# Attention and a gated feed-forward block on one core: adding two of the three terms of an approximated exponential on VectorE, with a new order plan

## The chip, the core and the metric

One core of a Trainium2 chip runs the kernel. The metric is the device time of one execution in microseconds. The kernel before has a median of 750.6 us over three runs (750.47 to 752.39).

The core has five engines, and the program gives each a queue of its own, in a fixed order: PE (TensorE, matrix multiplications from SBUF into PSUM), ACT (ScalarE, activation functions such as exp and tanh), DVE (VectorE, elementwise arithmetic), POOL (GpSimd) and SP (SyncE, which here only starts DMAs). The kernel uses PSUM as eight banks of 128 x 512 fp32 values (the tile PS).

## The reference

```python
# A_x: 1 x 2048 x 512, 32 heads of width 16; F = 1792
qkv = layernorm(A_x) @ A_wqkv
p = softmax(q @ k.T * 16 ** -0.5)          # per head, 2048 x 2048
h = A_x + (p @ v) @ A_wo
n = layernorm(h)
h2 = h + (sigmoid(n @ B_w_gate) * (n @ B_w_up)) @ B_w_down
```

The matrices of scores of the 32 heads have 2048 x 2048 x 32 elements, and each of them needs an exponential. That is most of what ACT does. The product with the values and the scores themselves are most of what PE does.

## The kernel before

**The unit of work.** A unit is a stretch of scores of 128 x 512 elements of one head: 128 keys on the partitions and 512 queries, or two blocks of 128 keys (SPAN is 2) and 256 queries. There are 2048 units. PE computes the scores of two or three units of one tile at once into neighbouring PSUM banks (`scores`, matmul at L1087): a head is only 16 wide, so the matmuls of different heads lie side by side in the array. There are 695 tiles. PE writes the scores of tile n+1 while tile n is turned into exponentials; the bank numbers alternate by the table PLACES (L1019), so scores of tile n+1 wait for those that read tile n-1.

**Two ways to an exponential.** Of each tile, ACT takes all units or all but one, in one activation of 512, 1024 or 1536 columns (L1415), and writes fp16 values into a place of the tile pt (or into other buffers that are free just then: xnT, QTb, xb, pe). The last unit of the tile can go to DVE (`dexp_first`, L1252): one tensor_scalar (L1258) writes a 16-bit integer whose bits, read as fp16, are a first approximation of the exponential. Two units share one buffer J (GQ is 2; six such buffers, QB). When both are there, `dexp_rest` (L1270) makes two further values of each from the first by adding an integer constant to the bits (the two "chords", CHORDS): POOL does this for both units at once as an int64_add over packed words (`chord64`, L1278), before POOL is free for it DVE does it (`chord`). The exponential is the sum of the three fp16 values, the last weighted by 1.5625 (through Vaug2, values that are weighted beforehand).

**The product with the values.** A unit of ACT is one row of value matmuls; a unit of DVE is three rows, since each of the three fp16 values is multiplied with the values (Vaug or Vaug2) and summed in PSUM (`av`, L1213, matmul at L1235). With SPAN 2 a row is two matmuls of 256 columns. The 17 columns of Vaug (16 values and a half for the row sum) are narrow, so the rows of four heads lie side by side, and four rows take the time of one. `avq` is the list of rows that wait, `todo` the number of rows still due for each head of a group; when it reaches zero, `finish_group` (L1113) transposes, divides by the row sum and transposes back on DVE.

**The rest of PE's work.** The projections of q, k and v, the product with A_wo and the feed-forward block (L826 gate and up, L844 down) are cut in pieces of two or four matmuls and put between the attention tiles (`try_bg`, L961), as fast as tokens come in. Where PE would be idle for too long, `stir` (L651) adds a matmul whose result nobody reads.

**What sets the order.** The kernel's Python code writes every queue out in one order while the program is built. It keeps a clock for each engine (T["P"], T["A"], T["D"], T["G"]) and books a cost for every instruction: 216 ns for a pass of PE, 112 for a change between kinds of matmul, for ACT 51 and 426.5 for each unit. Work for DVE, ACT and POOL waits as a `Job` (L523) until what it depends on is booked as done; `run_dve` (L599) picks the next job of DVE, `run_pool` (L552) that of POOL. In the main loop (L1377) each tile has an activation, perhaps a DVE unit, and then steps in which PE gets value rows or a dense piece. The dictionary PLAN (L23, 92 entries) overrides single choices: key 16 * tile + step forces what PE does in a step (1 to 3: so many rows of values, 4: a dense piece, 5: leave 100 ns, 9: end the tile), key + 15 forces (2) or forbids (1) a DVE unit, key + 14 chooses which head it takes.

**The tail** (L1487 on). After the last tile the remaining value rows, a first part of the last product with A_wo (identity part L1506, L1509), the last values, the last layernorm and the last feed-forward chunk follow: 14 steps of gate and up (L826), tanh (L856) and product (L839), then the down matmuls (L1584) and the output. At the very end three DVE instructions (L1593 to L1598) check all row sums for being in range, a matmul and a copy make one flag of it (L1601, L1603), and each engine reads the flag and branches: a general kernel follows if it is set, which it is not here.

Of the kernel before, what the change touches and what calls it, by code (L numbers as in the profile page):

```python
# [8 lines left out]
FP32 = mybir.dt.float32  # L9
# [13 lines left out]
PLAN = {414: 2, 528: 5, 656: 5, 672: 2, 736: 4, 737: 3, 750: 2, 769: 9, 801: 2, 815: 1, 817: 2, 1198: 3, 1200: 3, 1201: 3, 1376: 1, 1409: 3, 1423: 1, 1472: 9, 1473: 5, 1474: 4, 1601: 9, 1634: 3, 1682: 4, 1696: 9, 1713: 4, 1840: 9, 1857: 5, 1872: 4, 1873: 1, 1890: 9, 1938: 1, 2033: 1, 2047: 1, 2144: 5, 2145: 2, 2161: 2, 2384: 2, 2417: 4, 3728: 3, 3730: 4, 4240: 1, 4255: 1, 4321: 3, 4353: 4, 4367: 2, 4752: 2, 4753: 5, 4767: 2, 6112: 5, 6129: 3, 7040: 3, 7041: 3, 7696: 4, 7711: 1, 7713: 4, 7742: 2, 7761: 9, 7904: 2, 8512: 4, 8513: 3, 8913: 1, 8926: 3, 8928: 2, 8930: 1, 8943: 2, 8944: 4, 8960: 3, 8975: 1, 9200: 3, 9393: 4, 9410: 4, 9889: 4, 9890: 3, 9952: 2, 9984: 3, 10000: 2, 10178: 3, 10302: 2, 10528: 3, 10543: 2, 10640: 1, 10687: 2, 10703: 2, 10848: 4, 10894: 2, 10945: 1, 10959: 2, 11023: 1, 11089: 4, 11102: 1, 11103: 1, 11106: 1}  # L23
# [121 lines left out]
def kernel(  # L145
# [376 lines left out]
    T = {e: max(0.0, free[e] - tasks["go"].end) for e in free if e != "N"}  # L522
    class Job:  # L523
        def __init__(self, ns, fn, deps):
            self.ns, self.fn, self.deps, self.end = ns, fn, [d for d in deps if d is not None], None
# [5 lines left out]
        def place(self, eng):  # L531
            T[eng] = max(T[eng], self.ready()) + self.ns
            self.end = T[eng] + TAIL[eng]
            self.fn()
            if eng != "G":
                run_pool()
# [715 lines left out]
    def dexp_first(src, u, n):  # L1252
        if not half:
            half.append(dvx.tile([P, 3, GQ, QC], I16, name="J", bufs=QB))
            quads.append([])
        J = half[0]
        k = len(half) - 1
        nc.vector.tensor_scalar(out=J[:, 0, k, :], in0=src, scalar1=ZOFF, scalar2=float(-min(CHORDS)),  # L1258
                                op0=ALU.add, op1=ALU.max)
        T["D"] = max(T["D"], sc_end[n] + LAT) + 601  # L1260
        todo[u[0], u[1], u[3]] += 2
        uns = [Unit(u, J[:, s, k, :].bitcast(FP16), n, None if s else T["D"] + TAIL["D"],
                    v=Vaug2 if s == 2 else Vaug) for s in range(3)]
        avq.extend(uns)
        half.append(uns)
        quads[-1].extend(uns)
        if k == GQ - 1:
            dexp_rest()

    def dexp_rest():  # L1270
# [7 lines left out]
        def chord64(s):  # L1278
            nc.gpsimd.int64_add(words(s), words(0), CHORDS[s - 1] * (1 + 2 ** 16 + 2 ** 32 + 2 ** 48))  # L1279
            for i in range(k):  # L1280
                quad[i][s].end = T["G"] + TAIL["G"]
# [10 lines left out]
        for s in (1, 2):  # L1292
            if on_pool:
                pool(150 + 192 * k, lambda s=s: chord64(s), Mark(T["D"] + TAIL["D"]))
# [206 lines left out]
    while any(un.n < N - 1 and un.slot is not None for un in avq):  # L1501
        flush()
        av(8, 1e12)
    nc.scalar.activation(out=small.tile([P, 1], FP32, name="warm")[:], in_=eps_t[:], func=ACT.Sqrt)
    for i in range(n):
        nc.tensor.matmul(hps[i], lhsT=ident2[:], rhs=xl[:, i, :], start=True, stop=False)  # L1506
    for p in range(NP - 1):
        for i in range(n):
            nc.tensor.matmul(hps[i], lhsT=OT[qc, p][:, i * P:(i + 1) * P], rhs=wo_sb[:, p, :],  # L1509
                             start=False, stop=False)  # L1510
    T["P"] += MM * n * NP
# [12 lines left out]

    while avq:
        flush()
        av(8, 1e12)
    flush()
    mv = small.tile([P, n, nc.vector.BN_AGGR_DIM], FP32, name="mvl")
# [46 lines left out]
    hT = fpool.tile([P, FC, PW], BF16, name="hT")  # L1576
    for f in range(FC):
# [3 lines left out]
        glu_out(hT, f, tanh_out(g_ps[:, 0:CW[qc]]), u_ps[:, 0:CW[qc]])  # L1581
    for i in range(n):
        for f in range(FC):
# [6 lines left out]
    bad = small.tile([P, 1], FP32, name="bad")  # L1590
    okay = work.tile([P, S // 32 * NG], FP32, name="xs")
    rs = rsum[:]
    nc.vector.tensor_scalar(out=okay[:], in0=rs, scalar1=2 / SUM_HIGH, scalar2=None, op0=ALU.is_ge)  # L1593
    nc.vector.scalar_tensor_tensor(out=okay[:], in0=rs, scalar=2 / SUM_LOW, in1=okay[:],
                                   op0=ALU.is_le, op1=ALU.mult)
    nc.vector.tensor_reduce(out=bad[:], in_=okay[:], axis=AX.X, op=ALU.min)
    badb = small.tile([P, 1], BF16, name="badb")
    nc.vector.tensor_scalar(out=badb[:], in0=bad[:], scalar1=-1.0, scalar2=1.0, op0=ALU.mult, op1=ALU.add)  # L1598
    ones1 = small.tile([P, 1], BF16, name="ones1")
    nc.vector.memset(ones1[:], 1.0)  # L1600
    nc.tensor.matmul(acc[0:1, 0:1], lhsT=ones1[:], rhs=badb[:], start=True, stop=True)  # L1601
    flag = const.tile([1, 1], I32, name="flag")
    nc.vector.tensor_copy(out=flag[:], in_=acc[0:1, 0:1])  # L1603
# [34 lines left out]
```

## Time and profile before

| | |
|---|---|
| median of three runs | 750.6 us |
| the profiled execution | 750.78 us |
| span from its first to its last instruction | 749.0 us |
| PE busy, matmuls | 714.2 us, 11497 instructions |
| ACT busy | 710.6 us, 788 |
| DVE busy | 617.5 us, 1223 |
| POOL busy | 392.4 us, 715 |
| int64_add on POOL (L1279) | 646, mean 592 ns |
| first step of a DVE unit (L1258) | 611, mean 681 ns |
| activation of 128 x 1024 into pt (L1415) | 466, mean 1085 ns |
| granted TensorE clock | 0.998 |

Busy times add up the durations of single instructions. Instructions of one engine overlap in part: the next one starts before the profile calls the one before it ended, and up to four matmuls of narrow tiles run side by side. So a share of 95% doesn't say that the engine could do no more; the distance from start to start of two instructions that follow each other without a wait says what one of them costs. The first exponential starts at 13.06 us, the last ends at 714.68 us; what follows is the tail.

### The profile page before, as it was taken

The page shows a single profiled execution, that of the slowest core. Times are in us where ns is not written, and L with a number is a line of the kernel's source. Part 1 is how long each engine was busy: PE and PEld are TensorE (multiplying, and loading weights), DVE is VectorE, ACT ScalarE, POOL GpSimd, SP SyncE. Part 2 cuts the span into 40 slices and gives each one's busy share as a digit, 9 for nine tenths or more (in the row PEclk, how much of TensorE's full clock was granted, in tenths as well). Part 3 has the DMA queues.
Part 4 walks back from the last instruction along what each step waited for, and adds up shares of the span by engine and source line. Part 5 has one row for each costly group of instructions (what it writes and reads, how often), then busy time and mean ns, then how long its engine had stood idle before and what let it go on. Part 6 is the DMA issues. An engine that isn't in the chain of part 4 may idle for free.

```text
span 749.0 us, 27149 instructions
## 1 busy us (share of the span) xinstructions
PE 714.2 (95%) x11497; PEld 346.0 (46%) x11571; DVE 617.5 (82%) x1223; ACT 710.6 (95%) x788; POOL 392.4 (52%) x715
## 2 busy tenths in 40 slices
PE   8999998888999999999999999999999999999986
PEld 3322223444454445544555455535544455455554
DVE  7987898788988888898999678977889778898843
ACT  8988999999999999999999999999999999999952
POOL 2733556666565545664555545555564555566500
PEclk9999999999999999999999999999999999999999
DMA  7000005000132003311122123201321133003350
GB/s 239 1 1 1 1 2 170 2 3 3 31 101 76 20 10 101 87 31 30 45 63 68 37 65 99 61 9 39 101 58 37 31 93 115 10 10 87 97 173 18
DMA packets 68927, 41.65 MB, mean 56 GB/s; under 512 B 3520, under 2 KB 68800, under 8 KB 68800
## 3 DMA queue, kind: packets, MB, share of 16 engines
q1 hardware_dynamic: 68512, 39.59, 18.0%
q8 instruction: 92, 1.51, 0.9%
q14 instruction: 35, 0.29, 0.1%
q10 hardware_dynamic: 288, 0.26, 0.1%
HBM read 37.75 MB, written 2.10 MB: 53 GB/s over the span
## 4 chain that ended last, share of the span: by engine, by line
PE 71%; ACT 18%; DVE 6%; issue 4%; DMA 0%; POOL 0%; DVEq 0%; ACTq 0%; POOLq 0%
PE PS L1087 24%; PE PS L1235 22%; PE PS L826 13%; ACT pt L1415 12%; PE PS L844 5%; DVE J L1258 3%; PE PS L318 2%; ACT xnT L1415 2%; PE PS L765 2%; PE PS L313 2%; ACT pe L1415 1%; DVE xs L1153 1%; PE PS L1584 1%; ACT xb L1415 1%; ACT th L856 1%
## 5 line engine op out<-in xcount | busy, mean ns | idle before, releaser
L1279 POOL INT64_ADD J<-J x646 | 374.1, 592 | 303.4 <-DVE J L1258 253.0
L1415 ACT ACTIVATE pt<-PS 128x1024 f16<-128x1024 f32 (+1 forms) x516 | 520.8, 1119 | 9.2 <-PE PS L1235 4.8
L1258 DVE TENSOR_SCALAR J<-PS 128x512 int16<-128x512 f32 x611 | 408.4, 681 | 76.6 <-PE PS L1087 43.4
L1087 PE MATMUL PS<-QT,KT 32*128 32x256 bf16 (+1 forms) x3712 | 263.7, 276 | 13.6 <-ACT pt L1415 8.0
L1235 PE MATMUL PS<-J,Vaug 128*17 128x256 f16 (+1 forms) x3486 | 238.2, 279 | 2.0 <-DVE xs L1153 1.1
L1235 PE MATMUL PS<-pt,Vaug 128*17 128x256 f16 (+1 forms) x2049 | 195.6, 279 | 1.3 <-DVE xs L1153 1.0
L1087 PEld LDWEIGHTS <-KT 32*128 32x128 bf16 x3840 | 88.6, 92 | 197.7 <-issue 193.8
L1235 PEld LDWEIGHTS <-Vaug 128*17 128x17 bf16 x6164 | 138.4, 90 | 88.2 <-issue 82.5
L826 PE MATMUL PS<-xnT,wgu 128*128 128x256 bf16 x784 | 113.0, 275 | 0.2 <-DVE ob L850 0.2
L1415 ACT ACTIVATE xnT<-PS 128x1024 f16<-128x1024 f32 (+1 forms) x89 | 97.8, 1128 | 0.2
L826 PEld LDWEIGHTS <-wgu 128*128 128x128 bf16 x784 | 63.8, 98 | 38.9 <-issue 33.6
L1235 PE MATMUL PS<-xnT,Vaug 128*17 128x256 f16 x368 | 54.4, 273 | 0.0
L844 PE MATMUL PS<-wd,hT 128*128 128x512 bf16 x171 | 51.7, 383 | 2.3 <-issue 2.2
L1415 ACT ACTIVATE QTb<-PS 128x1024 f16<-128x1024 f32 x42 | 45.8, 1090 | 0.6 <-PE PS L1087 0.6
L856 ACT ACTIVATE th<-PS 128x512 f32<-128x512 f32 (+1 forms) x63 | 38.5, 612 | 7.9 <-DVE hT L839 6.1
L898 DVE SCALAR_TENSOR_TENSOR hT<-th,PS 128x512 bf16<-128x512 f32 x49 | 33.3, 680 | 6.2 <-PE PS L826 6.1
L1153 DVE STREAM_TRANSPOSE xs<-PS 128x256 f32<-128x256 f32 (+1 forms) x60 | 27.7, 461 | 10.8 <-PE PS L1235 10.3
L1235 PE MATMUL PS<-QTb,Vaug 128*17 128x256 f16 (+1 forms) x166 | 27.5, 275 | 0.4 <-DVE xs L1153 0.4
L1415 ACT ACTIVATE xb<-PS 128x1024 f16<-128x1024 f32 (+2 forms) x26 | 26.1, 1034 | 1.9 <-PE PS L1087 1.3
L1124 DVE TENSOR_TENSOR o<-xs,rsum 128x128 bf16<-128x128 f32 (+1 forms) x60 | 24.5, 408 | 2.1
L1415 ACT ACTIVATE pe<-PS 128x1024 f16<-128x1024 f32 (+2 forms) x22 | 21.9, 1068 | 1.5 <-PE PS L1235 0.9
L844 PEld LDWEIGHTS <-hT 128*128 128x128 bf16 x196 | 12.3, 97 | 20.8 <-issue 17.5
(128 smaller groups left out, 394.7 us busy)
## 6 DMA issues: line engine op xcount, KB each, us to landing
wgu<-in_B_w_gate_dram SPq DMA_DIRECT2D x49, 256.0 KB, 3.0
wgu<-in_B_w_up_dram SPq DMA_DIRECT2D x49, 256.0 KB, 3.4
out_dram<-ob SPq DMA_DIRECT2D x16, 128.0 KB, 1.7
wd<-in_B_w_down_dram SPq DMA_DIRECT2D x1, 1792.0 KB, 7.6
xr<-in_A_x_dram SPq DMA_DIRECT2D x14, 128.0 KB, 3.7
xb<-in_A_x_dram SPq DMA_DIRECT2D x6, 256.0 KB, 6.5
J<-in_B_w_gate_dram SPq DMA_DIRECT2D x4, 384.0 KB, 6.0
J<-in_B_w_up_dram SPq DMA_DIRECT2D x4, 384.0 KB, 6.8
```

Source lines behind the costliest of these rows:

```text
L313: nc.tensor.matmul(ps, lhsT=w_sb[:, d, p * P:(p + 1) * P], rhs=xnT[c][:, d, :], start=(d == 0), stop=(d == DC - 1))
L826: nc.tensor.matmul(ps[:, 0:PARTS[r][2]], lhsT=w[:, d, :], rhs=hn_of(r)[:, d, :], start=(d == 0), stop=(d == DC - 1))
L844: nc.tensor.matmul(ps, lhsT=hT[:, f, i * P:(i + 1) * P], rhs=wd[:, f, :], start=(f == 0), stop=(f == FC - 1))
L856: nc.scalar.activation(out=th[:, 0:ps.shape[-1]], in_=ps, func=ACT.Tanh, scale=0.5)
L898: nc.vector.scalar_tensor_tensor(out=hT[:, f:f + k, 0:w], in0=th[f][:].rearrange("p (k n) -> p k n", k=k), scalar=1.0, in1=ps2.rearrange(" ...
L1087: nc.tensor.matmul(pss[:, ui, i * CW[qc]:(i + 1) * CW[qc]], lhsT=KT[g // 2][32 * j:32 * j + 32, k * P:(k + 1) * P], rhs=q[32 * j:32 * j + ...
L1124: nc.vector.tensor_tensor(out=o2[:, 0:w // 32, DH * a:DH * a + DH], in0=xs[:, 0:w // 32, 0:DH], in1=rec.to_broadcast([P, w // 32, DH]), op ...
L1153: j = dve(650 - ns[0], lambda: nc.vector.transpose(out=xs[:, 0:w // 32, :].rearrange("p b r -> p (b r)"), in_=src), Mark(T["P"] + DRAIN), ...
L1235: nc.tensor.matmul(dst[32 * j:32 * j + VW, 0:w], lhsT=un.v[:, kt * SPAN[qc] + i, h, :], rhs=un.ap[:, i * w:(i + 1) * w], start=clears and ...
L1258: nc.vector.tensor_scalar(out=J[:, 0, k, :], in0=src, scalar1=ZOFF, scalar2=float(-min(CHORDS)), op0=ALU.add, op1=ALU.max)
L1279: nc.gpsimd.int64_add(words(s), words(0), CHORDS[s - 1] * (1 + 2 ** 16 + 2 ** 32 + 2 ** 48))
L1415: ex = nc.scalar.activation(out=pt, in_=pss[:, 0:wa, :], func=ACT.Exp, scale=AS)
```

## The change

Where a pair of DVE units goes to POOL, and DVE's list of ready jobs is empty at that moment (or PLAN says so: key + 12, 1 for yes and 2 for no), the pair's first value is added to the second on DVE, as an fp16 tensor_tensor over 1024 columns (512 for a single unit). The row of the first value is taken out of `avq` and of `todo`, so such a unit has two rows of value matmuls. POOL makes the second chord before the first for such a pair, and the add waits for the first. The value of the add is booked as ready when it is done; the first value of a pair without an add is now booked as ready when the pair is complete, not when it is written.

The bookkeeping learns that an add of DVE and an int64_add of POOL exclude each other (`lock`, `spans`, `holds`): each is booked behind the other if they would overlap. PLAN is new and has 354 entries over the whole run.

In the tail, the eight dense matmuls (identity and A_wo, now a list `fill`) no longer come ahead of the last value rows: rows that are ready go first, and the list fills the waits. The three checks of the row sums go between the steps of the last feed-forward chunk (after steps 2, 4, 6 and 8), the flag's matmul and copy after step 10.

```diff
         def place(self, eng):
-            T[eng] = max(T[eng], self.ready()) + self.ns
+            at = max(T[eng], self.ready())
+            if eng == "G":
+                for a, b in holds:
+                    if a <= at < b:
+                        at = b
+                spans.append((at, at + self.ns))
+            elif self.lock:
+                for a, b in spans:
+                    if a <= at + 40 and at < b - 150:
+                        at = b - 150
+                holds.append((at, at + self.ns))
+            T[eng] = at + self.ns
...
-        uns = [Unit(u, J[:, s, k, :].bitcast(FP16), n, None if s else T["D"] + TAIL["D"],
+        uns = [Unit(u, J[:, s, k, :].bitcast(FP16), n, None,
...
+        busy = sum(j.ns for j in dq if j.ready() is not None) + sum(c[0] for c in chain)
+        both = on_pool and (PLAN.get(16 * st["n"] + 12, 0) == 1 or PLAN.get(16 * st["n"] + 12, 0) == 0 and (busy == 0))
+        if both:
+            for uns in quad:
+                u = uns[0].u
+                avq.remove(uns[0])
+                todo[u[0], u[1], u[3]] -= 1
+
+            def add():
+                f1 = J[:, 1, 0:k, :].bitcast(FP16)
+                nc.vector.tensor_tensor(out=f1, in0=f1, in1=J[:, 0, 0:k, :].bitcast(FP16), op=ALU.add)
+                for uns in quad:
+                    uns[1].end = T["D"] + TAIL["D"]
+        else:
+            for uns in quad:
+                uns[0].end = T["D"] + TAIL["D"]
-        for s in (1, 2):
+        for s in (2, 1) if both else (1, 2):
             if on_pool:
-                pool(150 + 192 * k, lambda s=s: chord64(s), Mark(T["D"] + TAIL["D"]))
+                j = pool(150 + 192 * k, lambda s=s: chord64(s), Mark(T["D"] + TAIL["D"]))
+                if both and s == 1:
+                    dve(70 + 264 * k, add, j, pr=2).lock = True
...
-    while any(un.n < N - 1 and un.slot is not None for un in avq):
-        flush()
-        av(8, 1e12)
...
+    flush()
     while avq:
-        flush()
-        av(8, 1e12)
+        if av(8, 120.0):
+            flush()
+        elif fill:
+            fill.popleft()()
+            pe_time("dense", MM)
+        else:
+            flush()
+            av(8, 1e12)
...
+        if f in checks:
+            checks[f]()
+        if f == 10:
+            nc.tensor.matmul(acc[0:1, 0:1], lhsT=ones1[:], rhs=badb[:], start=True, stop=True)
+            nc.vector.tensor_copy(out=flag[:], in_=acc[0:1, 0:1])
```

## The prediction

> **What bounds the kernel now.** First the head of the page and its chain:
>
> ```profile
> PE 714.2 (95%) x11497; PEld 346.0 (46%) x11571; DVE 617.5 (82%) x1223; ACT 710.6 (95%) x788; POOL 392.4 (52%) x715
> ...
> PE 71%; ACT 18%; DVE 6%; issue 4%; DMA 0%; POOL 0%; DVEq 0%; ACTq 0%; POOLq 0%
> ```
>
> Two engines claim 95%, and the chain names mostly PE. A busy share can't settle it, so I read a stretch of the timeline, by start times:
>
> ```profile
> 300.12 0.62 PE L1235 MATMUL PS<-J,Vaug 128*17 128x256 f16 x16
> 300.68 0.40 PE L1087 MATMUL PS<-QT,KT 32*128 32x256 bf16 x6
> ...
> 301.57 0.40 PE L1087 MATMUL PS<-QT,KT 32*128 32x256 bf16 x6
> 301.90 0.61 PE L826 MATMUL PS<-xnT,wgu 128*128 128x256 bf16 x4
> 302.44 0.40 PE L1087 MATMUL PS<-QT,KT 32*128 32x256 bf16 x6
> ```
>
> and the same stretch on ACT:
>
> ```profile
> 301.15 1.94 ACT L1415 ACTIVATE pt<-PS 128x1024 f16<-128x1024 f32 x2
> 302.96 1.04 ACT L1415 ACTIVATE xnT<-PS 128x1024 f16<-128x1024 f32 x1
> 303.86 0.63 ACT L856 ACTIVATE th<-PS 128x512 f32<-128x512 f32 x1
> 304.34 4.74 ACT L1415 ACTIVATE pt<-PS 128x1024 f16<-128x1024 f32 x5
> ```
>
> ACT: from 301.15 to 302.96 it does two exponentials over 1024 columns, 0.905 us each; the tanh at 303.86 takes 0.48. Over the whole trace the commonest distances are 903, 1330 and 476 ns for 1024, 1536 and 512 columns, and these are also the smallest: ACT back to back. PE: scores take 0.33 us (one pass of 512 columns, 213 ns, and 112 for the switch of shape), four gate matmuls 0.54 (two passes and a switch), 16 value matmuls 0.56 (four run side by side, so two passes and 132 ns). A tile with two passes beside its scores thus takes 0.87 to 0.89 us of PE, and its exponential 0.90 of ACT. Both engines are nearly full.
>
> I priced every tile by these numbers, in the instruction order of both programs (us, tiles by number; the last tile of PE with its scores alone, what follows is the tail):
>
> | tiles | PE before | ACT before | PE after | ACT after |
> |---|---|---|---|---|
> | 0-74 | 72.3 | 67.3 | 71.1 | 68.2 |
> | 75-199 | 103.5 | 115.2 | 100.5 | 116.1 |
> | 200-449 | 248.2 | 246.3 | 242.7 | 245.4 |
> | 450-694 | 241.2 | 242.5 | 235.6 | 240.4 |
> | sum | 665.2 | 671.3 | 650.0 | 670.0 |
>
> The exponentials run from 13.06 to 714.68 us, 701.6. ACT needs 671.3 of it: 30.3 us are stalls, 13.7 before 200 us and 16.6 after. One kind is visible:
>
> ```profile
> 272.26 1.45 ACT L1415 ACTIVATE pt<-PS 128x1536 f16<-128x1536 f32 x1 [1.79 <-PE PS L1235]
> ```
>
> The exponential had no free place for its result, because PE was behind with the value matmuls that empty the places (L1344). PE's backlog becomes ACT's stall.
>
> **What the Trainium skill says.** "Perfetto Trace Analysis", in its opening note on judging how close a kernel is to roofline, calls matmul busy time a bad metric since matmuls are pipelined. The trace agrees: a gate matmul shows 275 ns, yet four of them and their switch pass in 540. "VectorE: DVE Perf Modes", The perf-mode tier table, gives a 16-bit tensor_tensor in SBUF at most two elements a cycle, 1224 ns for 2048; its side-by-side section splits that into some 158 cycles fixed and half a cycle per element. My estimate from that page for 1024: 670 cycles at 0.96 GHz, 0.70 us shown. No such row stands in this trace. "SBUF — State Buffer", Who interferes with whom: a VectorE instruction with two SBUF inputs and a GpSimd instruction that reads SBUF exclude each other, and the later one waits for all of the earlier. The trace has the sister case (a copy-like instruction, one input):
>
> ```profile
> L326 DVE TENSOR_SCALAR QT<-qd,mask x28: 328/344/747, 73.8 to 575.3; 128x512 bf16<-128x512 bf16 x28
> ```
>
> Alone it takes 344 ns; those that meet a running int64_add take up to 747, so a collision costs up to 0.4 us.
>
> **The change part by part.** ACT gets no new kind of work. The plan of the order grows from 92 to 354 entries, so every tile's place can shift; the table has that in it.
>
> *Value rows.* The new order holds 102 adds (92 over two units, 10 over one), so 194 of 614 VectorE units lose a row. Value matmuls fall from 6164 to 5810; in passes of 512 columns, four abreast, 812.25 to 762.5. 49.75 x 213 ns = 10.6 us of PE saved. Two warming matmuls less: 0.4. The new plan also groups PE's work in longer runs: 35 fewer groups (668 runs of scores instead of 674, 696 others instead of 725) at 112 to 132 ns, 4 us. Together 15, as the table's sums say.
>
> *Units.* VectorE takes 614 instead of 611, ACT 1434 instead of 1437: 1.3 us of ACT (the table).
>
> *Conversion.* ACT's 670 stays below everything, so PE's 15 us count only where PE is late. Scores run one tile ahead, thus PE and ACT can lag each other by some tiles. If I cut the order in groups of consecutive tiles and take the larger engine of each group, three tiles give 707.7 before and 696.6 after, four give 698.9 and 688.4. The measured 701.6 lies between, which fixes the depth. Gain by this sum: 10.5 to 11.1; I take 10.8. (One tile at a time it would be 17.5, twenty 8.6.)
>
> *The adds on VectorE.* Each is 0.60 us of engine time (0.70 shown, less about 0.09 by which neighbouring rows overlap: two L1258 of 0.68 fill 1.28), up to 1.3 us when it meets or awaits an int64_add (592 ns, L1279) in full. 102 x 0.6 to 1.3 = 61 to 133 us. Cover: from 200 to 700 us VectorE is 425 us busy with 836 instructions; less 0.09 each that is 350, so 150 of 500 is free, some 200 over the tiles. It fits, but not always at the right place. The new wait is the add's on POOL's chord; behind it on the in-order queue stands in 89 of 102 cases the next unit's L1258, which frees the score bank that PE's second next scores want. In 51 cases at most 1.2 us of VectorE work lie between the quad's last L1258 and the add, while POOL needs 2 x 0.6, so it will wait there, mostly at a moment when VectorE had nothing anyway (its largest wait now is for scores, 43.4 us). Bounds: 0 if always covered, 102 x 0.2 = 20 if each costs ACT a fifth of a microsecond. I take 1.5.
>
> *POOL and the buffers.* 642 int64_adds instead of 646 (374 us busy now), chord 2 before chord 1, and each can be held by an add. Covered: PE waited 0.2 us for POOL in all. A pair's rows now come an add later and none comes at once, so its J buffer (six pairs of units) is held longer; the new order still gives VectorE its 614 units, so I take nothing, and up to 1 us if PE runs out of ready rows.
>
> *Tail.* Now:
>
> ```profile
> 713.53 1.20 PE PS L1235 x36
> 714.73 0.54 PE PS L1506 x2
> 715.26 1.29 PE PS L1509 x6
> 716.56 0.36 PE PS L1235 x6
> ...
> 719.10 3.02 PE PS L844 x14
> 722.13 0.61 PE PS L307 x8
> 722.74 2.16 PE PS L844 x10
> 724.89 12.28 PE PS L826 x112
> ...
> 737.23 6.00 PE PS L1584 x27
> ```
>
> The last value matmuls wait behind eight dense ones (L1506, L1509), though the last exponential ends at 714.68. After, the dense ones follow and run under VectorE's transposes (716.95 to 718.45): 1.7 us gained. But the new order leaves 14 L844 instead of 10 ahead of L826: 4 x 0.216 = 0.9 lost. The flag checks (0.42, 0.69, 0.69, 0.16 us on VectorE) move between the 14 hT steps, which come every 0.93 us with 0.51 free: two of them exceed that by 0.18, 0.4 lost at most; the flag's matmul and cast (0.16 and 0.15) come into the same loop, 0.2. The flag is then ready before the last matmul, so PE loads it at 743.0 and not at 743.53, and the end, which follows PE's branch, comes 0.5 sooner. Net 1.7 - 0.9 - 0.4 - 0.2 + 0.5 = 0.7 gained. SP's eight loads into freed J buffers (L1519; issued from 707 to 716 us, 6 to 7 us to land) feed L826 from 724.7, so they have a microsecond of cover; that the last buffer comes free later would cost what exceeds it. The opening before the first exponential is the same.
>
> Sum: 10.8 + 0.7 - 1.5 = 10.0. The profiled execution took 750.78 us (span 749.0 and 1.8 around it); that leaves 740.8. The median of the runs is 750.6, 0.2 lower: 740.6.
>
> **Rivals.**
> - *Finer coupling.* If PE and ACT can't lag by more than a tile, the one-tile sum's 17.5 counts: 17.5 + 0.7 - 1.5 = 16.7, 733.9. For it: the plan now has entries for the whole run. Against: that sum gives 746 for a main part that takes 701.6.
> - *ACT decides alone.* If the stalls don't come from PE's load but from single late steps, only 1.3 + 0.7 remain: 748.6. For it: ACT is at its floor in most tiles. Against: the 1.79 us wait above ends on L1235.
> - *Slower: the add blocks the unit behind it.* An add held by POOL delays L1258, that the score bank, that the exponential two tiles on. It decides from 11.5/102 = 0.113 us of ACT per add; at 0.2 us, 750.6 - 11.5 + 20.4 = 759.5. For it: a strict queue, 89 units behind adds, and an int64_add that is running 53% of the time. Against: 200 us of free VectorE, and adds queued only when no job was ready.
>
> That the change does not happen is excluded: the order shows the adds and the missing rows.
>
> **Numbers.** Forecast 0.52; finer 0.18; ACT alone 0.14; blocked 0.16. About 0.3% (2.25 us) can be told from no change here. ACT alone lies on that border: 0.08 faster, 0.06 same. Faster 0.78, same 0.06, slower 0.16. The range 731 to 751 holds the first three but for the best of the second, and leaves most of the last out.
>
> **What would show it.** Right: PE's L1235 matmuls 354 fewer; ACT's distances still 903 ns, with stalls down from 30 to about 21; the add near 0.70 us; the eight dense matmuls behind the last value matmuls. Wrong: PE's L1087 or ACT waiting for J's first step or the add by more than 10 us in all, adds of over 1 us, or a stall total unchanged.

## The result, and the profile after

The changed kernel takes 747.9 us (median of four runs, 747.54 to 748.49), the kernel before beside it 750.59; the ratio is 0.9959 with a 95% interval of 0.9942 to 0.9977. So it is faster by 3 us, not by 10. The profiled execution took 747.74 us, with a span of 746.0.

The page after. The change adds 15 lines above the attention loop, so scores are now L1102, value matmuls L1250, the first step of a DVE unit L1273, int64_add L1294, the add L1318, the exponential L1449, gate and up L841, down L859.

```profile
PE 719.1 (96%) x11215; PEld 343.2 (46%) x11215; DVE 672.1 (90%) x1328; ACT 709.3 (95%) x788; POOL 418.6 (56%) x711
...
PE 60%; DVE 23%; ACT 10%; issue 3%; POOL 3%; POOLq 0%; DVEq 0%; ACTq 0%
...
L1294 POOL INT64_ADD J<-J x642 | 400.5, 637 | 271.8 <-DVE J L1273 217.4
...
L1273 DVE TENSOR_SCALAR J<-PS 128x512 int16<-128x512 f32 x614 | 405.0, 680 | 23.8 <-PE PS L1102 16.1
...
L1318 DVE TENSOR_TENSOR J<-J 128x1024 f16<-128x1024 f16 (+1 forms) x102 | 74.5, 730 | 9.7 <-POOL J L1294 9.0
```

Three things are to be seen. The value matmuls are fewer, as the order had said (5810 weight loads of L1250 on the page instead of 6164); that the busy time of PE is larger nevertheless comes from records that the trace of before lacks (171 of 196 L844 there, 196 here). DVE was 6% of the chain and is 23%, and the idle time ahead of its first steps fell from 76.6 to 23.8 us: most of the free time ahead of them is used up. And int64_add, the same instruction as before, went from 592 to 637 ns.

The line that showed what a collision on DVE costs stands a little higher in its median (344 ns before):

```profile
L326 DVE TENSOR_SCALAR QT<-qd,mask x28: 308/380/748, 76.1 to 572.6; 128x512 bf16<-128x512 bf16 x28
```

For ACT I take, as in the prediction, distances from start to start. Their smallest values are still 903, 1330 and 476 ns for 1024, 1536 and 512 columns. What goes beyond these is a stall. I put each stall in one of two classes: the exponential starts over 600 ns after its last score matmul ("place": it waited for a free place for its result) or sooner ("scores": it had to wait for the scores themselves). Worked out from the traces, in us (the last exponential is counted as 1.33 us long); "first step" is the mean distance, in ns, from the last score matmul of a tile to the start of its DVE step; the tail runs from the end of the last exponential to the end of the span:

| | exponentials, first start to last end | stalls | place | scores | first step late by | int64_add | tail |
|---|---|---|---|---|---|---|---|
| before | 701.4 | 29.9 | 7.8 | 19.4 | 635 ns | 592 ns | 34.5 |
| after | 699.0 | 28.9 | 0.7 | 25.3 | 707 ns | 637 ns | 33.5 |

(The two classes leave out stalls of under 30 ns each, some 3 us in all. After, the stall of 1.05 us at tile 133, where PE runs at half speed as told at the end, is counted with the scores.) The waits for places have all but vanished. Waits for scores have grown by 6 us, and the total is almost what it was. That was named in the prediction as a sign of being wrong.

Where a wait for scores comes from is seen in one stretch, first on DVE:

```profile
464.48 0.71 DVE L1139 TENSOR_TENSOR o<-xs,rsum 128x128 bf16<-128x128 f32 x1
465.12 1.09 DVE L1318 TENSOR_TENSOR J<-J 128x1024 f16<-128x1024 f16 x1
466.14 1.27 DVE L1273 TENSOR_SCALAR J<-PS 128x512 int16<-128x512 f32 x2
```

on POOL:

```profile
464.44 1.23 POOL L1294 INT64_ADD J<-J  x2 [0.26 <-DVE rsum L1138]
```

on PE:

```profile
466.37 0.86 PE L1102 MATMUL PS<-QT,KT 32*128 32x256 bf16 x6
```

and on ACT:

```profile
466.81 1.10 ACT L1449 ACTIVATE pt<-PS 128x1024 f16<-128x1024 f32 x1
468.17 1.02 ACT L1449 ACTIVATE xnT<-PS 128x1024 f16<-128x1024 f32 x1 [0.26 <-PE PS L1102]
```

The add starts at 465.12, while POOL's second int64_add runs until 465.67. It takes 1.09 us instead of 0.69, the first of the two first steps behind it starts at 466.14, the scores that need the bank of the first of them (six matmuls from 466.37) take 0.86 us instead of 0.40, and the second exponential on starts 1.36 us after the one before it, 0.46 above the floor.

Over the whole trace the exclusion follows one sum. The 37 adds over 1024 columns that start while an int64_add runs take longer than 0.69 us by what is left of it, less 0.15 us: with 0.264 us left the add takes 0.11 more, with 0.552 left 0.41 more. The other way round it is the same: an int64_add that starts 0.569 us before the end of an add takes 1.04 us instead of 0.61. Whichever comes second waits for nearly all that is left of the first.

The tail after, as the chain that ended last gives it:

```profile
711.72 1.64 POOL J L1294 x2
...
713.40 0.60 PE PS L1250 x10
714.00 0.54 PE PS L1535 x2
714.54 1.29 PE PS L1537 x6
715.83 0.43 PE PS L1571 x2
716.26 3.02 PE PS L859 x14
719.28 0.61 PE PS L307 x8
719.90 3.02 PE PS L859 x14
722.92 9.61 PE PS L841 x88
...
735.35 6.06 PE PS L1643 x28
```

The dense matmuls (L1535, L1537) now follow the last value matmuls, and 14 instead of 10 down matmuls stand ahead of L841, both as forecast. Ahead of the last value rows POOL stands in the chain: they wait for the last pair's chords.

### The profile page after: what moved, and what is told of

The parts are those of the page before. It is cut to its first block, busy times and chain, and to the rows that moved or that the text cites. A ratio compares the mean times of both kernels' runs of the same rounds, so it can differ in the third digit from the quotient of the medians.

```text
span 746.0 us, 26409 instructions
## 1 busy us (share of the span) xinstructions
PE 719.1 (96%) x11215; PEld 343.2 (46%) x11215; DVE 672.1 (90%) x1328; ACT 709.3 (95%) x788; POOL 418.6 (56%) x711
## 4 chain that ended last, share of the span: by engine, by line
PE 60%; DVE 23%; ACT 10%; issue 3%; POOL 3%; POOLq 0%; DVEq 0%; ACTq 0%
PE PS L1102 19%; PE PS L1250 17%; DVE J L1273 11%; PE PS L841 11%; ACT pt L1449 7%; PE PS L859 5%; POOL J L1294 3%; PE PS L313 2%; DVE J L1318 2%; DVE st L273 1%; DVE xs L1168 1%; PE PS L780 1%; PE PS L318 1%; DVE hT L913 1%; PE PS L474 1%
## 5 line engine op out<-in xcount | busy, mean ns | idle before, releaser
L1294 POOL INT64_ADD J<-J x642 | 400.5, 637 | 271.8 <-DVE J L1273 217.4
L1449 ACT ACTIVATE pt<-PS 128x1024 f16<-128x1024 f32 (+1 forms) x514 | 518.9, 1131 | 7.6 <-PE PS L1102 6.1
L1273 DVE TENSOR_SCALAR J<-PS 128x512 int16<-128x512 f32 x614 | 405.0, 680 | 23.8 <-PE PS L1102 16.1
L1102 PE MATMUL PS<-QT,KT 32*128 32x256 bf16 (+1 forms) x3712 | 266.1, 276 | 12.0 <-ACT pt L1449 7.5
L1250 PE MATMUL PS<-J,Vaug 128*17 128x256 f16 (+1 forms) x3140 | 222.2, 280 | 4.3 <-DVE xs L1168 3.5
L1250 PE MATMUL PS<-pt,Vaug 128*17 128x256 f16 (+1 forms) x2035 | 190.4, 280 | 1.1 <-DVE xs L1168 1.1
L1102 PEld LDWEIGHTS <-KT 32*128 32x128 bf16 x3840 | 90.6, 92 | 204.4 <-issue 199.9
L1250 PEld LDWEIGHTS <-Vaug 128*17 128x17 bf16 x5810 | 131.7, 90 | 84.5 <-issue 78.8
L841 PE MATMUL PS<-xnT,wgu 128*128 128x256 bf16 x784 | 111.9, 274 | 0.6 <-DVE hT L913 0.4
L1449 ACT ACTIVATE xnT<-PS 128x1024 f16<-128x1024 f32 (+1 forms) x91 | 100.8, 1140 | 0.4 <-PE PS L1102 0.3
L1318 DVE TENSOR_TENSOR J<-J 128x1024 f16<-128x1024 f16 (+1 forms) x102 | 74.5, 730 | 9.7 <-POOL J L1294 9.0
L841 PEld LDWEIGHTS <-wgu 128*128 128x128 bf16 x784 | 64.7, 97 | 38.1 <-issue 32.4
L1250 PE MATMUL PS<-xnT,Vaug 128*17 128x256 f16 x376 | 57.0, 273 | 0.4 <-DVE xs L1168 0.4
L859 PE MATMUL PS<-wd,hT 128*128 128x512 bf16 x196 | 56.5, 383 | 0.0
L1449 ACT ACTIVATE QTb<-PS 128x1024 f16<-128x1024 f32 x41 | 45.0, 1099 | 1.5 <-PE PS L1102 1.4
L1250 PE MATMUL PS<-QTb,Vaug 128*17 128x256 f16 (+1 forms) x162 | 27.8, 275 | 0.0
L1449 ACT ACTIVATE xb<-PS 128x1024 f16<-128x1024 f32 (+2 forms) x25 | 24.4, 1030 | 1.4 <-POOL xn L589 0.4
L1449 ACT ACTIVATE pe<-PS 128x1024 f16<-128x1024 f32 x24 | 23.5, 1036 | 1.5 <-PE PS L1102 1.5
```

The lines of the kernel that those rows point to most:

```text
L841: nc.tensor.matmul(ps[:, 0:PARTS[r][2]], lhsT=w[:, d, :], rhs=hn_of(r)[:, d, :], start=(d == 0), stop=(d == DC - 1))
L859: nc.tensor.matmul(ps, lhsT=hT[:, f, i * P:(i + 1) * P], rhs=wd[:, f, :], start=(f == 0), stop=(f == FC - 1))
L1102: nc.tensor.matmul(pss[:, ui, i * CW[qc]:(i + 1) * CW[qc]], lhsT=KT[g // 2][32 * j:32 * j + 32, k * P:(k + 1) * P], rhs=q[32 * j:32 * j + ...
L1250: nc.tensor.matmul(dst[32 * j:32 * j + VW, 0:w], lhsT=un.v[:, kt * SPAN[qc] + i, h, :], rhs=un.ap[:, i * w:(i + 1) * w], start=clears and ...
L1318: nc.vector.tensor_tensor(out=f1, in0=f1, in1=J[:, 0, 0:k, :].bitcast(FP16), op=ALU.add)
L1449: ex = nc.scalar.activation(out=pt, in_=pss[:, 0:wa, :], func=ACT.Exp, scale=AS)
```

## The experiments

Three theories are told apart in what was expected. V: the adds' time on DVE gives the gain back. A: ACT's stalls are single late steps that the order puts there, and PE's load has little to do with them. L: the add and int64_add exclude each other, and what one holds up on the other is what costs. Every ratio below is against runs of the kernel before on the same chip, with its 95% interval.

**The adds with nearly no work.** Everything as in the changed kernel, but each add touches 8 columns of each unit only.

```diff
-                nc.vector.tensor_tensor(out=f1, in0=f1, in1=J[:, 0, 0:k, :].bitcast(FP16), op=ALU.add)
+                nc.vector.tensor_tensor(out=f1[:, :, 0:8], in0=f1[:, :, 0:8],
+                                        in1=J[:, 0, 0:k, 0:8].bitcast(FP16), op=ALU.add)
```

> The changed kernel with its order, its waits and its 102 adds kept, but each add works on 8 columns of each unit and not on 512 (the rest of the first value is left out of the sum). VectorE is freed of about 102 x 0.6 = 60 us, PE and ACT have the same work. If VectorE's time for the adds gave the gain on PE back (theory V), the stalls of ACT shrink from about 30 to 20 us or less and the time falls from 747.9 to 738 to 742. If ACT's stalls come from single late steps whatever the load (theory A), it stays at 746.5 to 748. If the mutual exclusion with POOL is what costs (theory L), it falls as under V, since short adds hardly meet an int64_add; the next kernel tells these apart.

Measured: 743.21 us, ratio 0.9894 [0.9878, 0.9911]. The add's mean is 211 ns instead of 730, int64_add 599 instead of 637, the first step 565 ns late instead of 707, and the stalls 23.7 us. The adds as they are thus cost about 4.9 us (0.9959 - 0.9894, of 750.6), three times the 1.5 of the prediction. This alone doesn't tell V from L, since both time and collisions are gone.

**The time kept, the exclusion gone.** Two kernels put in place of the add an instruction of one SBUF input and about the same length, bn_stats over 512 fp16 values; the one reads the chord, so that it waits for POOL as the add did, the other the first value, so that it waits for nothing.

```diff
-                f1 = J[:, 1, 0:k, :].bitcast(FP16)
-                nc.vector.tensor_tensor(out=f1, in0=f1, in1=J[:, 0, 0:k, :].bitcast(FP16), op=ALU.add)
+                nc.vector.bn_stats(out=scr[:], in_=J[:, 1, k - 1, 0:k * QC // 2].bitcast(FP16))
```

(in the second kernel `J[:, 0, ...]`.)

> The changed kernel with its order, but each of the 102 adds is replaced by a bn_stats over 512 (256) elements of the second value: it waits for POOL's chord as the add does, takes about the same 0.6 us of VectorE, but has one input from SBUF and so needn't exclude POOL (the first value is left out of the sum). Theory V: 746.5 to 748, as the changed kernel. Theory L: 740 to 743, with the int64_adds back at 592 ns from 637. Theory A: 746.5 to 748.

Measured with the wait: 744.27 us, ratio 0.9897 [0.9876, 0.9918].

> The changed kernel with its order, each add replaced by a bn_stats over 512 (256) elements of the first value: 0.6 us of VectorE, no wait for POOL and no exclusion (the first value is left out of the sum). If the exclusion with POOL costs the 4 us that a_nolock won back: as a_nolock, 743 to 745. If waiting for POOL's chord costs too (9.0 us of VectorE's idle time in the changed kernel): 741 to 743. If only VectorE's time costs: it can't be faster than a_nolock by more than the spread of runs.

Measured without it: 743.45 us, ratio 0.9909 [0.9887, 0.9932]. The groups of this second kernel, the one on POOL:

```profile
L1295 POOL INT64_ADD J<-J x642 | 376.6, 600 | 290.4 <-DVE J L1274 233.2 <-DVE rsum L1139 18.0 <-DVE nw L292 11.3
```

the one on DVE (shortest, median and longest in ns):

```profile
L1318 DVE BATCH_NORM_STATS2 scr<-J x102: 400/682/694, 61.1 to 706.9; 128x6 f32<-128x512 f16 x92, 128x6 f32<-128x256 f16 x10
```

and, for comparison, that of the add in the changed kernel:

```profile
L1318 DVE TENSOR_TENSOR J<-J x102: 397/692/1141, 61.4 to 711.8; 128x1024 f16<-128x1024 f16 x92, 128x512 f16<-128x512 f16 x10
```

The medians are the same, 682 and 692; only the add has a long end. The DVE time is kept, yet 3.7 to 4.7 us come back, as much as with the add's work taken away within the intervals. So where the plan has a place for it, the time on DVE is nearly free, and so is the wait for the chord; the exclusion costs 4 to 5 us. V falls for the planned order, L stands. One more thing differs with bn_stats: no value row waits for its result, as rows do for the add's. That is not where the time is, for in the kernel with 8 columns the rows still wait for the add, and PE's waits for the add in the changed kernel come to 0.2 us.

Tile by tile, the cost is not spread over the 102 adds. Beside the second of these kernels, 16 of the 695 exponentials in the changed one wait longer by 0.1 to 0.6 us each, 4.6 us together (one of them is tile 133, where the clock told at the end has a part). Five of them, with 1.8 us, come at most 3.5 us behind an add of 1.09 to 1.14 us; the longest extra wait, 0.61 us at 94.74 us, follows the add of 1.09 us at 92.78.

**Work on DVE that nobody planned.** The kernel before, with 102 such bn_stats of the first value put on DVE at moments when its queue is empty, without being booked.

```diff
+        busy = sum(j.ns for j in dq if j.ready() is not None) + sum(c[0] for c in chain)
+        st["ld"] = st.get("ld", 0) + (on_pool and busy == 0)
+        if on_pool and busy == 0 and st["ld"] % 7 < 5:
+            nc.vector.bn_stats(out=scr[:], in_=J[:, 0, k - 1, 0:k * QC // 2].bitcast(FP16))
```

> The kernel before, its order unchanged, with 102 bn_stats of 0.6 us added on VectorE, each right behind the second unit of a pair when VectorE's list of ready jobs is empty; nobody waits for their results and PE's work stays as it was. Theory V: the same load costs here what it cost in the change, 6 to 10 us: 757 to 761. Theory A or L: VectorE has 150 us to spare, so 750 to 753.

Measured: 757.37 us, ratio 1.0089 [1.0069, 1.011]: 6.7 us for 102 x 0.67. The stalls rise from 29.9 to 36.5, all of it in the class of scores (the first step comes 765 ns late). V is right in an order that doesn't know of the work. Empty at the moment of the decision is not free.

**PE's relief alone.** The kernel before with 424 value matmuls left out, spread over the run, nothing else touched. What was expected counts them as 53 passes; some are 512 columns wide and not 256, so by columns they are 55, 55 x 213 ns = 11.7 us.

```diff
+                if (st.get("owed", 0) > 0 and len(row) == 4 and st["row"] % 14 < 7
+                        and all(count[r.u[:2] + (r.u[3],)] > 1 and todo[r.u[:2] + (r.u[3],)] > 2 for r in row)):
+                    skip.update(id(r) for r in row)
...
-            for i in range(SPAN[qc]):
+            for i in range(0 if id(un) in skip else SPAN[qc]):
```

> The kernel before, its order unchanged, with 53 whole passes of value matmuls left out over the run (424 matmuls, so those rows are missing from the sums): 11.3 us less for PE, nothing else changed. If PE's load makes ACT's stalls (the prediction's conversion, theory V needs it too): 739 to 743. If ACT decides alone (theory A): 748 to 751.

Measured: 747.92 us, ratio 0.9958 [0.9944, 0.9972]: 3.2 us for 11.7, 0.27 us per us. The large wait for a place that the prediction showed as PE's backlog is still there; of ACT's waits by releaser in this kernel:

```profile
ACT pt L1432 <- PE PS L1252: 4.1, 4, 1.8
```

Before, that line had 4.8 us in 5 waits, the longest 1.8 as well. From start to start that wait shrinks from 1.96 to 1.51 us above the floor. So it is mostly a matter of where the order puts the rows of one particular place, and less of how much PE has to do. That is theory A, for the order of before.

**PE's load added.** To see whether the quarter holds in both directions and in both orders, value matmuls are issued twice: 432 in the kernel before (by columns 56 passes, 11.9 us) and 412 in the changed one (53 passes, 11.3 us).

```diff
+                if (st.get("owed", 0) > 0 and len(row) == 4
+                        and all(count[r.u[:2] + (r.u[3],)] > 1 and todo[r.u[:2] + (r.u[3],)] > 2 for r in row)):
+                    twice.update(id(r) for r in row)
...
-            for i in range(SPAN[qc]):
+            for i in [x for x in range(SPAN[qc]) for _ in range(2 if id(un) in twice else 1)]:
```

> The kernel before with 54 passes of value matmuls issued twice (432 matmuls, 11.5 us of PE), spread as in the run on the changed kernel; the doubled products are added twice, so the output differs from the reference. Counterpart to the 53 passes left out. By the sum: 750.6 + 11 = 762. By the quarter: 753.5. If load costs more than relief brings, because every tile that is full now becomes late, it lies between, 756 to 760.

Measured: 760.74 us, ratio 1.0131 [1.0116, 1.0147]: 9.8 us for 11.9, 0.82 us per us, a little above the 756 to 760 that were expected for a load that costs more than relief brings.

> The changed kernel with 52 passes of value matmuls (four heads abreast, 412 matmuls, 52 x 213 ns = 11.1 us of PE) issued twice, spread evenly over the run; order, adds and all else as in the changed kernel. The doubled products are added twice, so the output differs from the reference. This puts back the PE work that the adds save, but keeps the new order. If PE's relief is worth what my sum by groups of tiles said, about 1 us per us: 748 + 10 = 758. If it is worth the quarter that leaving out 53 passes in the old order gave: 748 + 3 = 751, and the new order itself must then bring the rest of the gain. If stalls don't depend on PE's load at all: 748.

Measured: 755.91 us, ratio 1.0065 [1.0052, 1.0079]: 8.0 us above the changed kernel (1.0065 - 0.9959) for 11.3, 0.71 us per us. Its profile has a fall of the TensorE clock in tiles 10 to 19 that the profile of the changed kernel has not; with these tiles left out, its stalls are larger by 7.0 us (table below), 0.62 us per us.

So load counts at 0.82 us per us in the old order and relief at 0.27: the order of before was tight for just its load. Theory A alone, by which load should count little too, falls. The new order is tight for its smaller load, and with the rows' work (and 1 to 2 us more) put back it is 4.9 us slower than before: the adds and the order cost, the rows pay.

**The tail alone.** The kernel before with the tail of the changed one, nothing else.

> The kernel before with the edit of the tail alone (the dense matmuls behind the last value rows, the checks between the last steps). The traces of before and of the change put the distance from the last exponential to the end at 34.5 and 33.5 us. All theories: 0.7 to 1.7 us faster, 749.3 to 750.3 beside a before of 751.0.

```diff
-    while any(un.n < N - 1 and un.slot is not None for un in avq):
-        flush()
-        av(8, 1e12)
+    fill = [lambda i=i: nc.tensor.matmul(hps[i], lhsT=ident2[:], rhs=xl[:, i, :], start=True, stop=False)
+            for i in range(n)]
...
+        if f in checks:
+            checks[f]()
```

Measured: 748.24 us, ratio 0.9965 [0.9951, 0.9979]. Its chain in the tail:

```profile
716.88 0.43 PE PS L1537 x2
...
723.10 9.61 PE PS L826 x88
...
735.53 6.06 PE PS L1609 x28
741.59 0.02 issue
741.61 0.60 ACT ob L1612
```

Beside the kernel before (724.89 for L826, 737.23 for the down matmuls): 1.8 us from the dense matmuls, 12.43 instead of 12.34 us from L826 to the down matmuls, so the checks and the flag cost 0.1, and the end comes 4.1 us after the last output activation (span 746.3) instead of 5.2. Together 2.7 us in the profile (the exponentials end 0.1 earlier) and 2.6 by the runs, where 0.7 to 1.7 were expected. In the order of before the edit of the tail is thus worth nearly as much as the whole change; inside the change it is worth 1.0 us.

**The plan of before under the new code.** The changed kernel with the PLAN of before; and the same with the adds neither issued nor booked and the rows left out all the same (464 matmuls fewer than before; the first value's share of the sums is missing).

```diff
-PLAN = {65: 5, 97: 2, ...
+PLAN = {414: 2, 528: 5, ...
...
-                if both and s == 1:
-                    dve(70 + 264 * k, add, j, pr=2).lock = True
```

(the last two lines only in the second kernel.)

> The changed kernel with the plan of before (92 entries): 96 adds where VectorE's list is empty, 338 value matmuls fewer, 611 units on VectorE as before, but no lookahead. Theory V (adds cost VectorE, PE's relief is worth little by itself): 749 to 754, no gain over before. If the adds carry the gain and the plan adds nothing: 747 to 748.5, as the changed kernel.

Measured: 759.53 us, ratio 1.0118 [1.0101, 1.0135], with 96 adds and 338 value matmuls fewer than before.

> As d_oldplan, but the adds are neither issued nor booked (the first value is left out of the sum; rows are dropped as with the adds). The order comes out anew: 464 value matmuls fewer than before and 630 units on VectorE. Theory V: VectorE's time is what the adds use up, so this gains on PE, on ACT (19 units, 8 us) and pays nothing: 736 to 742. Theory A, in which loads decide little: ACT's 8 us and the tail, 741 to 743; a result above 744 speaks against both.

Measured: 745.76 us, ratio 0.9934 [0.9917, 0.995]. A result above 744 was said to speak against both theories, and it does. The order that comes out is another one: 46 passes of value matmuls fewer (9.8 us of PE), and 630 units on DVE instead of 611, which takes about 8 us of work off ACT. Of the 5.0 us some 1.5 are the tail's (33.0 us instead of 34.5), so both together bring 3 to 4: the exponentials run for 697.5 us instead of 701.4, and ACT's stalls rise from 30 to 34. Most of what is taken off is lost again in an order that was not planned for it. The kernel with the 96 adds is 13.8 us slower, an upper figure for what they cost there (it also does 126 value matmuls more, and 19 units more on ACT). The new plan takes 11.6 us from 759.5: without it the change would have been slower.

**Whose exclusion it is.** The add walks its operands in steps of two elements, even ones first; same sum, same order.

```diff
-                f1 = J[:, 1, 0:k, :].bitcast(FP16)
-                nc.vector.tensor_tensor(out=f1, in0=f1, in1=J[:, 0, 0:k, :].bitcast(FP16), op=ALU.add)
+                f0, f1 = (J[:, s, 0:k, :].bitcast(FP16).rearrange("p a (n t) -> p a t n", t=2) for s in (0, 1))
+                nc.vector.tensor_tensor(out=f1, in0=f1, in1=f0, op=ALU.add)
```

> The changed kernel with the add's two inputs and its output walked in steps of two elements (even ones, then odd ones); same sum, same order. If the exclusion with POOL belongs to any instruction of two SBUF inputs: int64_add stays at 637 ns mean or gets longer, the add goes to 1.1 us or more if the stride makes it slower, and the time to 752 or more. If the exclusion belongs to the fast mode of 16-bit operands alone: add 1.1 us, int64_add back at about 600 ns, and the time is 748 plus what 102 x 0.45 us of VectorE cost without a place in the plan (6.7 us for 0.67 each before, so up to 4.5) less 4 for the exclusion: about 748 to 749. If the stride costs nothing: 748 and unchanged rows.

Measured: 802.25 us, ratio 1.0702 [1.0681, 1.0723], 50 us beyond the 752 that were named as the least for this case. The groups on POOL and the add's:

```profile
L1294 POOL INT64_ADD J<-J x642 | 447.4, 710 | 278.9 <-DVE J L1273 224.9 <-DVE rsum L1138 18.2 <-DVE nw L291 13.2
```

```profile
L1318 DVE TENSOR_TENSOR J<-J x102: 718/1366/1823, 61.0 to 764.7; 128x1024 f16<-128x1024 f16 x92, 128x512 f16<-128x512 f16 x10
```

The stride doubles the add (1366 instead of 692 ns), and int64_add gets longer still: 710 ns mean, the longest 2093. So the exclusion is not one of the fast form of the add; it goes with an add of two SBUF inputs in either form, for as long as it runs. That is what the Trainium skill says ("SBUF — State Buffer", Who interferes with whom: the port pair that both engines share is an exclusive lock), and this trace and the two with bn_stats agree. The stalls rise from 28.9 to 81.3 us, and the first step comes 950 ns late. My expectation had counted the longer add as DVE time at the price of the unplanned bn_stats and was off by 50: 0.67 us of DVE more per add cost 0.55 us of the end (1.0702 - 0.9959, of 750.6, by 102). How much of that is DVE's time and how much exclusion, this run does not separate.

**The last pairs.** The changed kernel with adds forbidden from tile 686 on, so that the last value rows don't wait for a pair.

```diff
+PLAN.update({16 * n + 12: 2 for n in range(686, 700)})
```

> The changed kernel with adds forbidden from tile 686 on (2 adds and 8 value matmuls' difference), all else the same. If the tail loses because the last pair's value is ready late (the value matmuls wait for POOL's chord and the dense ones follow), the time from the last exponential to the end goes down by up to 1 us, to 747; otherwise 748.

Measured: 747.4 us, ratio 0.9947 [0.9934, 0.9961]; its interval overlaps that of the changed kernel. The tail of its profile is 33.0 us instead of 33.5. This is inconclusive; its five runs spread from 745.79 to 750.48 for a likely reason that the last section gives. No version here that computes the whole result beats the changed kernel beyond doubt.

The stalls of all kernels whose order could be matched tile by tile, leaving out tiles 10 to 19, where some executions have the disturbance told at the end:

| | stalls without tiles 10-19, us |
|---|---|
| before / tail alone | 29.2 / 29.1 |
| passes left out / issued twice, old order | 26.3 / 38.8 |
| unplanned work on DVE | 35.8 |
| after | 27.1 |
| add on 8 columns / bn_stats with wait / without wait | 21.9 / 22.5 / 22.7 |
| after with passes twice | 34.1 |
| strided add | 79.6 |

The three kernels without the exclusion agree within a microsecond, and 4.4 to 5.2 us below the changed one.

## Why the prediction was right and wrong

**What held.** The direction; the 354 matmuls, the add's price where it meets nothing (692 ns median, 0.70 forecast), ACT's floors, the eight dense matmuls behind the last values, 14 down matmuls instead of 10.

**"The adds on VectorE: I take 1.5."** This step failed. Without exclusion the kernel is 3.7 to 4.9 us faster, so the adds cost about 4.4, some 0.043 us each in the mean. The prediction had the collision in it (0.4 us in L326), counted free time on DVE against it and concluded that it fits. But the cover is not free time in sum: 38 of the 102 adds start while an int64_add runs, and a delay goes on to the first step queued behind it, to the score bank, and to ACT two tiles on. Most delays are absorbed on the way; 16 exponentials carry the loss. The collisions also lengthen POOL: 642 x (637 - 600) ns = 24 us; how much of the loss comes by that way, no run separates. This is the chain of the rival "the add blocks the unit behind it", at a fifth of the 0.2 us that the rival gave each add.

**"Conversion: gain 10.5 to 11.1; I take 10.8."** This step failed too. With the exclusion taken away the exponentials run for 694.5 us (without wait) or 693.7 (8 columns) instead of 701.4: a gain of 6.8 to 7.6 us, with ACT's own 1.3 and the adds' DVE time (in the former) in it. Three things are known of the 3 to 4 us that are missing. First, the rows save less PE time. The 49.75 passes count all value matmuls as four abreast. In the trace of before a run of 18 value matmuls takes 777 ns and one of 24 takes 776, when the head with the most rows has three in both: the fullest head sets the time. Counted so, the passes up to the last scores fall from 830 to 786, 44 x 213 ns = 9.4 us and not 10.6. Secondly, the halved clock told below stalls ACT at tile 133, by 0.7 and 0.9 us in these two kernels. Thirdly, the step took one curve, the larger engine in each group of tiles, for relief and load alike. In the old order the runs show a bend at the point for which it was planned: 0.82 us per us of load, 0.27 per us of relief. What relief brings thus depends on the plan, which the sum does not hold. About 2 us of what is missing are not taken apart. The rows' worth in the new order was measured only from the loaded side (7.0 to 8.0 us for 11.3, so some 6 to 7 for 9.4), and no run isolates the 4 us of fewer changes between kinds of matmul.

By the profiles the whole comes to this: 6.8 us gained on the exponentials without the exclusion, 4.5 lost to it again (699.0 instead of 694.5), 1.0 gained in the tail, and 0.36 lost in a longer opening (first exponential at 13.42 us instead of 13.06), which I had taken as the same. That gives 2.9, and the spans differ by 3.0.

**"PE's backlog becomes ACT's stall."** Right for load, wrong as the explanation of the wait for a place at 272.26: 1.51 of its 1.96 us survive 11.7 us of relief, and it goes only where the order is another one. The prediction's own sign, stalls from 30 to 21, was nearly fulfilled by the kernels without exclusion (23.7 and 24.4), not by the change.

**The tail, 0.7.** Right within a third: 1.0 in the profile (34.5 to 33.5). By terms: dense matmuls behind the values 0.75 instead of 1.7, since the last value rows now wait for POOL's chord (711.72 to 713.36); 14 instead of 10 down matmuls -0.86 (forecast -0.9); checks and flag -0.1 instead of -0.6; the end after the last output activation 4.0 us instead of 5.2, a gain of 1.2 instead of 0.5.

**The rivals.** "ACT decides alone" gave 748.6 and came nearest in number, but its reason is not what happened: a gain of some 7 us on the exponentials and a loss of 4.5 to the exclusion stand behind the number. "Finer coupling" had more conversion, where there was less.

## What to carry to other kernels

Before giving an idle engine a new instruction, ask not only whether its time fits but whom it locks out while it runs: here 102 adds of 0.69 us were nearly free as time and cost 4 to 5 us as collisions with POOL, and the same adds without a plan that knew of them cost up to 14. In a kernel whose order was planned for its load, a us more on the tight engine costs nearly a us and a us less brings a quarter until the order is planned anew; a gain must be measured with the new order, and its cost with the old. Split off the unrelated edit: alone, in the order of before, that of the tail brings 2.6 us, where the whole change brings 3.1.

## What the runs showed of the hardware that I had not expected

The TensorE clock. In the changed order PE runs at half speed for 3.4 us near 145 us (value passes of 256 columns start 0.2 us apart from 143.99 on, and 0.1 apart from 146.9 on), and in every profile of that order for 3.4 or 6.8 us somewhere between 142 and 156 us. The windows of the kernel after, with the granted clock third from the right:

```profile
140.00:145.00 5.00, 3.46 (x66) 1.80 (x64) 4.17 (x8) 5.00 (x6) 3.46 (x6) 0.85 0.00 0
145.00:150.00 5.00, 4.61 (x96) 2.33 (x85) 3.90 (x9) 4.01 (x6) 2.76 (x5) 0.81 0.02 3
```

and before:

```profile
140.00:145.00 5.00, 3.95 (x79) 2.21 (x75) 2.68 (x5) 5.00 (x6) 2.65 (x6) 1.00 0.01 3
145.00:150.00 5.00, 4.41 (x89) 2.03 (x90) 4.24 (x9) 5.00 (x6) 3.19 (x6) 1.00 0.02 3
```

ACT's stall at tile 133, 1.05 us, stands there. In some executions of the new order the clock also falls between 24 and 33 us; in the profile of the kernel without adds at the end:

```profile
24.00:28.00 4.00, 3.49 (x17) 1.02 (x14) 2.89 (x8) 2.93 (x4) 3.50 (x7) 0.68 0.00 0
28.00:33.00 5.00, 4.75 (x24) 1.91 (x23) 3.09 (x7) 2.16 (x3) 1.72 (x3) 0.57 0.01 2
```

There four matmuls of 512 columns take 1.91 us instead of 1.03, and the stalls of tiles 10 to 19 are 4.5 us instead of 1.8. This is in the profiles of three kernels in the new order (the one with bn_stats and a wait, that with passes twice, and this one). It would explain why runs of the new order spread by up to 4.7 us and those of the old by 2.3 at most: in the five runs of the kernel without adds at the end, times of 745.8, 746.0, 747.4, 747.7 and 750.5 us go with mean granted clocks of 0.999, 0.999, 0.997, 0.995 and 0.991.

The Trainium skill ("TensorE: Matmul & The Clock Gate", Part 1) names the half clock as the state after a window of some 3.4 us without activity. The half rate and the length agree: by the clock records of the trace it lasts 3.41 us (143.47 to 146.88), in other profiles 3.41 or 6.83. But PE was not idle before it. Busy time shows no difference: from 139 to 142 us PE is busy for 2.36 of 3 us after and 2.38 before. Another count does. If each matmul is taken as its columns times 213/512 ns, and those that run side by side are counted once, PE streams columns for 35% of the 3.41 us ahead of the drop, 140.06 to 143.47, and for 60% of the same stretch in the kernel with the tail alone, whose order is that of before. Cut from there into pieces of 3.41 us, the trace of after has no lighter one between 15 and 720 us; the next has 52%. With bn_stats and no wait the numbers are 35% and 54%. So a light stretch of PE goes with the drop. Why not every light stretch brings one is open (the strided kernel has drops after 42, 45 and 50%, and two pieces of 47% without one), and no experiment moved the light stretch. The kernel with passes left out has no such drop.

Smaller ones: an fp16 add of two SBUF inputs over 1024 columns takes 0.69 us where it meets nothing, one in steps of two elements 1.35; and an add over 16 values in place of 1024 still takes a median of 165 ns.
